# An attention kernel with a hand-made plan: the value groupings of its windowed half go by DMA on the SP queue instead of copies on VectorE, and eps is added as a per-row scalar

## The chip, the cores and the metric

The kernel runs on one core of one Trainium2 chip. The time is device microseconds (us) of that core. Three executions of the kernel before gave 351.57, 351.86 and 356.25 us; the median, 351.86 us, is the time to compare with. A further execution was profiled: it took 352.71 us, and 350.6 us of that is the span that the profile covers.

## The reference, cut to what matters

Two attention layers, A and B, work on a sequence of 2048 rows with D = 640, 32 heads and 20 values a head. Their results stand side by side in the output.

```
# A: causal softmax attention inside each of 4 segments of 512 rows,
#    and a memory (M, z) of the segments before
a_dot = softmax(q k^T * scale + causal mask) v
a_mem = (phi(q) M) / (phi(q) z + 1e-06)        # phi(t) = t + 1 if t > 0 else exp(t)
o = g * a_mem + (1 - g) * a_dot                # g = sigmoid(beta), one per head
M, z = M + phi(k)^T v, z + sum(phi(k))
# B: every row i looks at the rows j with 0 <= i - j < 256
o = softmax(where(mask, q k^T * scale, -1e9)) v
out = concat([o_A @ A_wo, o_B @ B_wo], axis=-1)
```

## The kernel before, in words

**Chunks.** The work is cut into eight chunks of 512 rows, in the order A0, B0, A1, B1, A2, B2, A3, B3. While the scores of one chunk run, the projections of the next one (q, k and v) are worked in between. Heads are taken four at a time: eight groups, 0 to 7.

**A chunk's path.** TensorE computes q and k (`qk_job`, line 416) and v (`v_job`, line 550) into two PSUM banks named `m`, and VectorE evicts them (lines 445, 568, 573). The last 12 rows of each quarter of q and k are regrouped through DRAM by DMAs on the SP queue (`regroup`, lines 400 and 408); they make the groups 5 to 7. Scores go to three PSUM pairs named `sc` (line 631), ScalarE turns them into `pt` tiles by exp (line 647; 12 such tiles in a ring), GpSimd zeroes what the mask excludes (line 682), or VectorE does, for the window's ends (line 664). TensorE multiplies by the values (lines 696 and 717), VectorE transposes the result (line 748), takes reciprocals (line 774), GpSimd divides (line 782). For A's memory, the denominators get eps added first (line 768), then a reciprocal (line 772), a product on VectorE (line 793) and a sum on GpSimd (line 802). The finished rows go to DRAM (line 820), come back transposed by DMA (line 835), are multiplied by wo (line 735) and stored (line 906).

**B's values.** A window of 256 rows makes a tile of 128 queries look at half a tile of keys at both ends. The halves of two different tiles are put together in one 128-row operand. For this, `v_ends` (line 583) makes three further groupings of the value tile `vB`: `vL` (the lower 64 partitions of four tiles), `vU` (the upper 64 partitions) and `vX` (the upper 64 of this chunk's first tile above the lower 64 of the last chunk's). It runs after each of the two halves of the heads, `half` 0 and 1: three VectorE copies each time, and for half 0 of a chunk that has one before it two more, that carry the last chunk's values over. This makes 30 copies in the program, all on line 601. `half` 0 covers the columns 0 to 335, `half` 1 the rest. Line 697 reads 32 columns from 21 h on for head h, so the last head of group 3 (h = 15) reads columns 315 to 346, and with them 11 of half 1.

**What sets the order.** The program has no loop at run time. A planner (`Flow`, line 58) keeps a clock of its own for every engine, adds the cost that each call states (`on_dve(402.0)`, for example), and issues at each point what its clocks say is ready. `when_idle` puts a VectorE job off until VectorE's planned time allows it; `at` issues at a planned time; `mark` says when a result is there, and the value product of a group waits, in the plan, for the mark "v" of that group (lines 1157 and 1160). Each engine then runs its instructions strictly in the planned order, with semaphores for the true dependences. A change of one stated cost so can move instructions on every engine. DMAs are spread over eight completion semaphores; one that reuses a semaphore waits until the earlier transfer on it has landed (the planner's `LANES`, line 47).

Of the kernel before, what the change touches and what calls it, by code (L numbers as in the profile page):

```python
# [9 lines left out]
ALU = mybir.AluOpType  # L10
# [3 lines left out]
P = 128  # L14
H = 32
DH = 20
# [168 lines left out]
class _K:  # L185
# [397 lines left out]
    def v_ends(self, n, c, half, v):  # L583


        f = self.f
        lo, hi = slice(0, SH), slice(SH, P)
        w = 16 * VS
        s = slice(0, w) if half == 0 else slice(w, VW)
        todo = []  # L590
        if half == 0 and c > 0:
            pv = self.vB[(c - 1) % 2]
            todo += [(self.vU[hi, 0:2, :], pv[hi, 2:4, :], 580.0),
                     (self.vX[lo, :], pv[lo, 0, :], 380.0)]
        todo += [(self.vL[lo, :, s], v[lo, :, s], 610.0),
                 (self.vU[hi, 2:4, s], v[hi, 0:2, s], 320.0),
                 (self.vX[hi, s], v[hi, 0, s], 430.0)]
        left = [len(todo)]
        for out, in_, ns in todo:
            def go(out=out, in_=in_, ns=ns):  # L600
                self.nc.vector.tensor_copy(out=out, in_=in_)
                t = f.on_dve(ns)
                left[0] -= 1
                if left[0] == 0:
                    for g in range(4 * half, 4 * half + 4):
                        self.mark(t, n, "v", g)
            f.when_idle(f.dve + 138.0, go)

    def v_tile(self, name, now=True):
        v = self.big.tile([P, LT, VW], BF16, name=name)  # L610
# [142 lines left out]
    def norm(self, turned, dst, add_to, last, g=None):  # L753


        nc, f = self.nc, self.f
        tt, slot, t0 = turned
        NB = L // HD
        tv = tt[:].rearrange("p (b c) -> p b c", c=HD)
        rr, rslot = self.piece("rr", NTT, 1, F32, (P, NB))  # L760
        a, b = tv[:, :, 0:DH], rr[:].unsqueeze(2).to_broadcast([P, NB, DH])
        if len(dst.shape) == 4:
            a = a.rearrange("p (g b) d -> p g b d", g=4)
            b = b.rearrange("p (g b) d -> p g b d", g=4)

        def s1():
            if add_to:
                nc.vector.tensor_tensor(out=rr[:], in0=tv[:, :, DH],
                                        in1=self.eps[:, g:g + 1].to_broadcast([P, NB]),
                                        op=ALU.add)  # L770
                f.on_dve(100.0, t0)
                nc.vector.reciprocal(out=rr[:], in_=rr[:])
            else:
                nc.vector.reciprocal(out=rr[:], in_=tv[:, :, DH])  # L774
            t1 = f.on_dve(276.0, t0)
            if add_to:
                f.when_idle(t1, lambda: s3(t1))
            else:
                f.at(t1 - 100.0, lambda: s2(t1))

        def s2(t1):
            nc.gpsimd.tensor_tensor(out=dst, in0=a, in1=b, op=ALU.mult)  # L782
            t2 = f.on_pool(QPOOL, t1)
            self.done_with(slot, t2)
            self.done_with(rslot, t2)
            if last:
                last(t2)

        def s3(t1):
            while len(self.adds) >= 2:  # L790
                self.adds[0]()
            u, uslot = self.piece("u", 2, 1, BF16, (P, NB, DH))
            nc.vector.tensor_tensor(out=u[:], in0=a, in1=b, op=ALU.mult)
            t = f.on_dve(480.0, t1)
            self.done_with(slot, t)
            self.done_with(rslot, t)

            def add():
                if add not in self.adds:
                    return  # L800
                self.adds.remove(add)
                nc.gpsimd.tensor_tensor(out=dst, in0=dst, in1=u[:], op=ALU.add)  # L802
                t3 = f.on_pool(717.0, t)
                self.done_with(uslot, t3)
                if last:
                    last(t3)
            self.adds.append(add)
            f.at(t, add)

        f.when_idle(t0, s1)  # L810

    def final(self, n, o, scr, wo, out2d, r0, col, t0, t1, t):
# [549 lines left out]
```

## Time and profile before

| what | value |
|---|---|
| median of three executions | 351.86 us |
| profiled execution, its span | 352.71 us, 350.6 us |
| busy: PE / ACT / POOL / DVE | 326.4 / 315.0 / 294.3 / 278.2 us |
| exp on ACT (line 647) | 320 instructions, 296.6 us |
| value copies on DVE (line 601) | 30 instructions |
| eps added on DVE (line 768) | 24 instructions, 7.8 us |
| granted TensorE clock | 1.00 in every stretch |
| data moved by DMA | 40.54 MB, 45.2% of 16 engines' span on queue q1 |

PE is TensorE's matmuls, ACT is ScalarE, POOL is GpSimd, DVE is VectorE, SPq is the SP engine's queue, which issues nearly all DMAs. A busy PE is not one at its peak, since matmuls are pipelined. The durations of ACT rows overlap a little with the next row: in a run of exps their starts lie about 0.9 us apart (23 exps in the 20.00 us from 108 to 128), while one row reads 1.07 us on average. In the columns of a stretch, each engine's number is its busy time inside the stretch, with the instructions in brackets.

### The profile page before, as it was taken

To read this page: it belongs to the slowest core of one execution; us is meant where nothing else is said; L and a number is where in the kernel's file an instruction comes from. 1 tells how busy PE (TensorE), PEld (TensorE's weight loads), DVE (VectorE), ACT (ScalarE), POOL (GpSimd) and SP (SyncE) were. 2 spreads that over 40 slices of the span, in tenths; PEclk is the share of its full clock that TensorE was granted. 3 is DMA by queue.
4 is the path that set the end of the run, shared out by engine and by line. 5 is a ranking of instruction groups with operands and counts; after the bars stand their busy time and mean duration, and the time that the engine had idled before them with its cause. 6 is when DMAs were issued, how large, how long until landed. Compare 5 with 4: busy or idle time off the path is not lost.

```text
span 350.6 us, 13578 instructions
## 1 busy us (share of the span) xinstructions
PE 326.4 (93%) x5617; PEld 167.0 (48%) x5617; DVE 278.2 (79%) x557; ACT 315.0 (90%) x358; POOL 294.3 (84%) x592
## 2 busy tenths in 40 slices
PE   7999999989999999999999999988999999899994
PEld 2443435444544345455644436454543445566672
DVE  5687677999958999999967998997867999766621
ACT  2897499999999999999999999999999999989831
POOL 6589388988898989999898989899988989987720
PEclk9999999999999999999999999999999999999999
DMA  7945617526675133033794025030483032675773
GB/s 233 376 159 129 165 32 227 128 64 178 200 124 123 22 77 122 2 93 69 175 193 104 0 63 155 3 79 8 82 143 77 2 75 61 146 140 150 146 183 115
DMA packets 69374, 40.54 MB, mean 116 GB/s; under 512 B 48448, under 2 KB 67520, under 8 KB 69312
## 3 DMA queue, kind: packets, MB, share of 16 engines
q1 hardware_dynamic: 67584, 38.35, 45.2%
q10 hardware_dynamic: 1728, 1.32, 1.2%
q8 instruction: 44, 0.72, 0.9%
q14 instruction: 18, 0.15, 0.1%
HBM read 16.06 MB, written 16.38 MB: 93 GB/s over the span
## 4 chain that ended last, share of the span: by engine, by line
PE 48%; DVE 22%; POOL 11%; issue 6%; ACT 5%; DMA 5%; SPq 2%; DVEq 0%; ACTq 0%; POOLq 0%
PE m L735 30%; PE sc L631 9%; POOL pt L682 7%; PE m L696 6%; ACT pt L647 5%; DVE tt L748 4%; DVE pt L664 3%; DMA xT<-in_B_x_dram 2%; PE m L717 2%; DMA scr_o<-o 2%; POOL o L782 2%; DVE kB L445 1%; PE sc L735 1%; DVE pq L471 1%; DVE qA L445 1%
## 5 line engine op out<-in xcount | busy, mean ns | idle before, releaser
L647 ACT ACTIVATE pt<-sc 128x1024 bf16<-128x1024 f32 (+1 forms) x320 | 296.6, 1070 | 14.9 <-PE sc L631 12.9
L682 POOL TENSOR_SCALAR_AFFINE_SELECT pt<-pt 128x256 bf16<-128x256 bf16 x448 | 209.6, 495 | 36.0 <-ACT pt L647 30.8
L748 DVE STREAM_TRANSPOSE tt<-m 128x512 f32<-128x512 f32 x88 | 60.7, 706 | 19.4 <-PE m L696 9.4
L782 POOL TENSOR_TENSOR o<-tt,rr 128x320 bf16<-128x320 f32 x64 | 51.2, 801 | 2.8 <-DVE rr L774 2.7
L631 PE MATMUL sc<-qB,kB 20*64 20x64 bf16 (+2 forms) x1728 | 39.0, 217 | 1.2 <-issue 0.6
L735 PEld LDWEIGHTS <-xT 128*128 128x128 bf16 x320 | 28.7, 97 | 22.4 <-issue 11.6
L735 PEld LDWEIGHTS <-oT 128*128 128x128 bf16 x320 | 28.8, 97 | 17.2 <-issue 3.5
L631 PE MATMUL sc<-qA,kA 20*128 20x128 bf16 (+3 forms) x512 | 36.1, 300 | 0.9 <-ACT pt L647 0.3
L631 PEld LDWEIGHTS <-kB 20*64 20x64 bf16 (+1 forms) x1728 | 21.7, 98 | 25.1 <-issue 23.1
L735 PE MATMUL m<-wv_A,xT 128*128 128x320 bf16 x160 | 27.4, 300 | 3.7 <-DVE kA L445 2.0
L891 DVE CAST ot<-m 128x320 bf16<-128x320 f32 x46 | 21.9, 480 | 8.5 <-PE m L735 8.3
L735 PE MATMUL m<-xT,wq_A 128*128 128x512 bf16 x100 | 26.6, 386 | 1.1 <-DVE qA L445 0.9
L664 DVE TENSOR_TENSOR pt<-pt,ends 128x1024 bf16<-128x1024 bf16 x32 | 27.6, 875 | 0.0
L735 PE MATMUL m<-xT,wk_A 128*128 128x512 bf16 x100 | 27.2, 392 | 0.3
L735 PE MATMUL m<-xT,wBq 128*128 128x512 bf16 x100 | 25.8, 380 | 1.2 <-DVE tt L748 1.2
L735 PE MATMUL m<-xT,wBk 128*128 128x512 bf16 x100 | 25.3, 381 | 0.6 <-DVE kB L445 0.6
L735 PE MATMUL m<-wBv,xT 128*128 128x320 bf16 x160 | 25.6, 300 | 0.3 <-DVE tt L748 0.2
L631 PEld LDWEIGHTS <-kA 20*128 20x128 bf16 x512 | 10.5, 91 | 30.5 <-issue 29.8
L696 PE MATMUL m<-pt,vA 128*32 128x128 bf16 (+3 forms) x512 | 24.0, 302 | 0.5 <-POOL pt L682 0.3
L735 PE MATMUL m<-wo_A,oT 128*128 128x320 bf16 x120 | 20.8, 300 | 0.2 <-DVE ot L891 0.2
L802 POOL TENSOR_TENSOR o<-o,u 128x320 bf16<-128x320 bf16 x24 | 20.5, 854 | 0.0
L445 DVE CAST qB<-m 128x512 bf16<-128x512 f32 x20 | 13.6, 682 | 7.4 <-PE m L735 7.4
(87 smaller groups left out, 427.7 us busy)
## 6 DMA issues: line engine op xcount, KB each, us to landing
scr_o<-o SPq DMA_DIRECT2D x28, 160.0 KB
out_dram<-ot SPq DMA_DIRECT2D x27, 160.0 KB
xT<-in_B_x_dram SPq DMA_DIRECT2D x4, 720.0 KB
scr_pk<-e SPq DMA_DIRECT2D x15, 128.0 KB
xT<-in_A_x_dram SPq DMA_DIRECT2D x3, 640.0 KB
scr_kA<-kA SPq DMA_DIRECT2D x16, 60.0 KB
scr_qA<-qA SPq DMA_DIRECT2D x16, 60.0 KB
kA<-scr_kA SPq DMA_DIRECT2D x16, 60.0 KB
```

Of the source, the lines that this page charges most:

```text
L445: nc.vector.tensor_copy(out=dst[:, m, at:at + L], in_=ps[:, :])
L631: nc.tensor.matmul(ps[j // 2][h0:h1, j % 2, c0:c0 + nq], lhsT=k[rows, g, kc + h0:kc + h1], rhs=q[rows, g, q0:q0 + nq], start=True, stop=Tr ...
L647: nc.scalar.activation(out=pt[:, :, lo:hi], in_=ps[i][:, :, lo:hi], func=ACT.Exp, scale=self.scale)
L664: nc.vector.tensor_tensor(out=blk, in0=blk, in1=self.ends[:].unsqueeze(1).to_broadcast([P, 1024 // SH, SH]), op=ALU.mult)
L682: nc.gpsimd.affine_select(out=blk, in_=blk, pattern=pat, compare_op=ALU.is_ge, fill=self.zero, base=base, channel_multiplier=mul)
L696: nc.tensor.matmul(O[HD * j:HD * j + HD, q0:q0 + nq], lhsT=v[:, VS * h:VS * h + HD], rhs=pts[j // 2][:, j % 2, c0:c0 + nq], start=(n_ == 0 ...
L717: nc.tensor.matmul(O[HD * j:HD * j + HD, o0:o0 + nq], lhsT=v[:, VS * h:VS * h + HD], rhs=pts[j // 2][:, j % 2, c0:c0 + nq], start=(n_ == 0 ...
L735: self.nc.tensor.matmul(ps[:, 0:n], lhsT=lhsT, rhs=rhs, start=start, stop=stop)
L748: self.nc.vector.transpose(out=tt[:], in_=O[:, :])
L782: nc.gpsimd.tensor_tensor(out=dst, in0=a, in1=b, op=ALU.mult)
L802: nc.gpsimd.tensor_tensor(out=dst, in0=dst, in1=u[:], op=ALU.add)
L891: nc.vector.tensor_copy(out=ot[:, 320 * hf:320 * hf + 320], in_=ps[:, 0:320])
```

## The change

In `v_ends`, the copies on VectorE become DMAs from SBUF to SBUF on the SP queue. All of one half are issued together, at the planned time at which VectorE has evicted the values; the order inside is now `vL`, `vU`, `vX`, and the two carried pieces last. The mark "v" is set from the planned landing of the last DMA. In `norm`, the eps of A's memory is no longer a tensor that is broadcast along the row, but the per-row scalar of a tensor_scalar; the planned cost stays 100 ns.

```diff
@@ v_ends @@
-        todo = []
+        todo = [(self.vL[lo, :, s], v[lo, :, s], 820.0),
+                (self.vU[hi, 2:4, s], v[hi, 0:2, s], 410.0),
+                (self.vX[hi, s], v[hi, 0, s], 205.0)]
         if half == 0 and c > 0:
             pv = self.vB[(c - 1) % 2]
-            todo += [(self.vU[hi, 0:2, :], pv[hi, 2:4, :], 580.0),
-                     (self.vX[lo, :], pv[lo, 0, :], 380.0)]
-        todo += [(self.vL[lo, :, s], v[lo, :, s], 610.0),
-                 (self.vU[hi, 2:4, s], v[hi, 0:2, s], 320.0),
-                 (self.vX[hi, s], v[hi, 0, s], 430.0)]
-        left = [len(todo)]
-        for out, in_, ns in todo:
-            def go(out=out, in_=in_, ns=ns):
-                self.nc.vector.tensor_copy(out=out, in_=in_)
-                t = f.on_dve(ns)
-                left[0] -= 1
-                if left[0] == 0:
-                    for g in range(4 * half, 4 * half + 4):
-                        self.mark(t, n, "v", g)
-            f.when_idle(f.dve + 138.0, go)
+            todo += [(self.vU[hi, 0:2, :], pv[hi, 2:4, :], 820.0),
+                     (self.vX[lo, :], pv[lo, 0, :], 410.0)]
+        t = f.dve + 138.0
+
+        def go():
+            for out, in_, ns in todo:
+                self.nc.sync.dma_start(out=out, in_=in_)
+                tl = f.on_dma(1, ns, t)
+            for g in range(4 * half, 4 * half + 4):
+                self.mark(tl, n, "v", g)
+        f.at(t, go)
@@ norm, s1 @@
             if add_to:
-                nc.vector.tensor_tensor(out=rr[:], in0=tv[:, :, DH],
-                                        in1=self.eps[:, g:g + 1].to_broadcast([P, NB]),
-                                        op=ALU.add)
+                nc.vector.tensor_scalar(out=rr[:], in0=tv[:, :, DH],
+                                        scalar1=self.eps[:, g:g + 1], scalar2=None,
+                                        op0=ALU.add)
                 f.on_dve(100.0, t0)
```

## The prediction, as it was put on record

> **What bounds the kernel now.** I read the page's busy shares first:
>
> ```profile
> PE 326.4 (93%) x5617; PEld 167.0 (48%) x5617; DVE 278.2 (79%) x557; ACT 315.0 (90%) x358; POOL 294.3 (84%) x592
> ```
>
> Four engines are near each other, so the shares decide nothing. The second view is the table by stretches: from the first exp of B0 (41.14) to the end of the last exp (332.03), then the places where the 30 copies lie, then the last chunk (columns: us, then busy time of PE, PEld, DVE, ACT, POOL).
>
> ```profile
> 41.14:332.03 290.89, 275.18 (x5183) 142.30 (x5182) 244.78 (x498) 284.53 (x321) 263.62 (x513) 1.00 0.44 100
> 116.00:124.00 8.00, 7.56 (x84) 2.66 (x82) 7.77 (x17) 8.00 (x10) 7.65 (x15) 1.00 0.22 33
> 131.00:137.00 6.00, 5.84 (x152) 3.87 (x148) 5.47 (x11) 6.00 (x7) 6.00 (x13) 1.00 0.61 188
> 199.00:204.00 5.00, 5.00 (x45) 1.79 (x46) 4.82 (x12) 5.00 (x7) 4.56 (x10) 1.00 0.04 5
> 212.00:217.00 5.00, 4.83 (x90) 2.87 (x87) 4.42 (x9) 5.00 (x7) 5.00 (x10) 1.00 0.76 221
> 277.00:282.00 5.00, 5.00 (x51) 1.83 (x48) 4.82 (x11) 5.00 (x6) 4.45 (x10) 1.00 0.00 0
> 290.00:297.00 7.00, 6.92 (x160) 3.91 (x160) 6.32 (x14) 7.00 (x8) 7.00 (x15) 1.00 0.21 63
> 301.00:332.00 31.00, 28.71 (x935) 19.00 (x928) 19.93 (x42) 28.88 (x31) 25.25 (x57) 1.00 0.71 158
> ```
>
> ScalarE is busy 284.53 of 290.89 us and 36.00 of the 36.00 us of the six stretches with copies. It is the bound. Its work (320 exps, 30 exps for phi) is untouched by the change, and its idle time between 41.14 and 332.03 is 290.89 - 284.53 = 6.36 us. That is all a faster VectorE can give back there. VectorE itself is nearly full in the copy stretches (7.77 of 8.00, 4.82 of 5.00), which makes the copies look dear; but it isn't what ScalarE waits for.
>
> The third view is the chain that ended last, in its last 20 us (start, length, what):
>
> ```profile
> 333.53 0.80 PE m L717 x63
> 334.32 1.48 PE sc L735 x10
> ...
> 338.58 0.57 SPq L820
> ...
> 339.19 2.50 DMA scr_o<-o
> ...
> 341.81 3.49 DMA oT<-scr_o
> ...
> 345.35 1.54 PE sc L735 x10
> ```
>
> After the last exp the end is a chain of the SP queue: transposes of the last chunk's first three tiles, then the last rows' store, their transpose, ten matmuls. The fourth view is the SP queue in the last A chunk, where the new DMAs go:
>
> ```profile
> 281.21 1.55 SPq L400 DMA_DIRECT2D scr_kB<-kB  x4
> 285.34 1.42 SPq L408 DMA_DIRECT2D kB<-scr_kB  x4
> 286.80 1.64 SPq L400 DMA_DIRECT2D scr_qB<-qB  x4
> 290.65 1.42 SPq L408 DMA_DIRECT2D qB<-scr_qB  x4
> 294.13 5.03 SPq L906 DMA_DIRECT2D out_dram<-ot  x2
> ```
>
> The queue is idle for most of that time. By the waits of the queue, line 400 waited 15.6 us here for the last value copy.
>
> **The change, part by part.**
>
> *Copies removed.* The groups by shape have two ends among the copies:
>
> ```profile
> L601 DVE COPY vU<-vB 64x1368 bf16<-64x1368 bf16 x3 | 1.9, 648 | 0.1
> ...
> L601 DVE COPY vX<-vB 64x336 bf16<-64x336 bf16 x4 | 1.0, 245 | 0.1
> ```
>
> The eight shapes sum to 2.3 + 2.3 + 2.0 + 1.9 + 1.9 + 1.8 + 1.8 + 1.0 = 15.0 us of VectorE. What hides them is ScalarE's exps: it has no idle time in these stretches. If that cover were gone, the 15.0 us would show in full. Worth on the path: at most 6.36 us (all of ScalarE's idle time from 41.14 on), and at least nothing; it could not make things worse by itself. I take -0.5, near the lower end, since the only idle of ScalarE around copies is that of the stretch from 128 to 165 (36.29 busy of 37.00: 0.7 us).
>
> *Eps.* 24 tensor_tensors of 323 ns (7.8 us) become tensor_scalars. The nearest rows are line 352 (128x32, 172 ns) and line 467 (128x512 bf16, 371 ns). So VectorE gains 24 x 0.15 = 3.6 us or loses 24 x 0.05 = 1.2. They lie in the A chunks beside saturated exps: taken 0 on the path, ends -0.7 (the same idle) and +1.2 (if nothing hid the loss).
>
> *DMAs added on SP.* 30 issues: 2 x 3 for B0 and 2 x 3 + 2 for each of the other three. The queue's issues above take 1.55/4 = 0.39 us each, so 12 us of SP, in gaps of 4 to 16 us. Data: each half has 64 x 7 pieces of 672 to 696 bytes, 0.30 MB, and the carried pieces 0.26 MB three times; 3.2 MB in all beside 40.54 MB. Landing: the stores of line 400 end their issue at 282.76 and the next line that needs them starts at 285.34, so 2.6 us. What waits for them: in the changed order half 0 stands before the stores of kB (line 400), half 1 after the return of qB. In the last chunk half 1 is issued from 292.07 on, for 3 x 0.39 us, and lands at about 292.07 + 1.2 + 2.6 = 295.9; its first reader on PE runs at 301.31, 5.4 us later, and in B0 to B2 it is no tighter (group 0 needs only half 0; first readers at 65.4, 142.7, 224.0). B0's half 1 is now queued behind the 720 KB load of xT, which takes until 63.6 by the chain; it lands at about 66, and group 3, its first reader, comes some 10 us later. Half 0 is no later than its cast; line 400, queued behind it, waited for the last copy before and now waits for the cast only, some 2 us sooner, against 5 x 0.39 = 2.0 us of issues that fall into its wait. Taken 0; ends -0.7 and +4.1 (the first rival).
>
> On the SBUF page of the Trainium skill ("SBUF — State Buffer", Door 1) a rule speaks against such transfers: 64 partitions reach only 8 of the 16 ports, and 196 GB/s was measured on partitions 0 to 63. An estimate by it and by the fixed 2.0 us of "DMA: Bandwidth & Descriptors" (Anatomy of one DMA) is 0.30 MB / 196 GB/s + 2.0 = 3.5 us in place of the 2.6 us of this trace. The sum is the same by both, since 5.4 us are there; no run here has yet shown a 64-partition transfer.
>
> *Order.* The planner now sees less VectorE time and shifts matmuls between neighbouring score batches from about 58.6 us on (the first: a set of 84-wide matmuls now ahead of the 64 end scores). Instruction counts on PE, ACT and POOL stay equal. What such a plan costs is unknown. Nearest row: the longest wait of an exp for PE after 41.14 is 1.01 us, at 308.32. Ends: -6.36 (all idle gone) and +7.1 (one such wait more in each of the seven chunks after A0). I take 0, the middle of errors of both signs.
>
> *Tail.* In the changed order, five matmuls of the chunk before last stand after the last value product. The first of the three transposes reuses the buffer that they read, and so waits for them: 334.32 + 5 x 0.148 = 335.1, where before it was issued at 334.62 (by then a store of line 906, now moved behind, had held the queue until 334.53). From there the chain above is the same: +0.5. Ends -0.7 (if the moved store counts and PE's wait of 1.41 us before 345.35 covers the five) and +1.5 (two times the five matmuls).
>
> Sum: -0.5 + 0 + 0 + 0 + 0.5 = 0.0 against the profiled execution's 352.71. The median of the runs is 0.85 us below that; I predict 352.3, between the two.
>
> **The rivals.**
>
> *Slower: the regrouping of q and k is pushed back by the transfers ahead of it.* Place: last chunk. Its 64-wide scores of all eight groups start at 295.09 and need the q rows issued until 292.07, landing at 294.7: 0.4 us of slack (in the other chunks these scores come for two groups at a time, so groups 5 to 7 are needed late). Five transfers now precede the kB stores. If the stores are issued more than 0.4 us later than at 281.21, PE stands still and ScalarE after it. Price: 5 x 0.39 us of issues plus 0.56 MB at 221 GB/s (the rate of the stretch 212 to 217), 2.5 us, less 0.4: up to +4.1, so 356.8. For it: line 400 waited for the last copy. Against: the casts of kB come earlier.
>
> *Slower: the new order.* ScalarE's feed has three PSUM pairs and is paid for in waits of 0.2 to 1.0 us. If the order adds one wait of 1.01 us in each of seven chunks: +7.1, 359.8; from three such waits on it outweighs the rest. For it: the order was made with costs in which a transfer takes 205 to 820 ns, which nothing in the trace confirms. Against: the same planner made the order before, with 6.36 us of idle.
>
> *Faster: VectorE matters more than ScalarE's busy time shows.* If the freed 15.0 + 3.6 us of VectorE let PE run ahead and remove most of the waits: -5, 347.7. For it: PE waits on VectorE's evictions at many small places. Against: it can't pass 6.36 us, and none of that lies in the copies' stretches.
>
> **How the numbers follow.** No change within a few us (350 to 355): 0.53. Regrouping late (354 to 357): 0.12. Order (355 to 362): 0.19, of it 0.14 above +2%, that is above 358.9. VectorE (345 to 350): 0.13, of it 0.04 below -2%, that is below 344.8. 0.03 is left for things unseen, 0.01 of it faster by over 2%, 0.02 slower. So: faster 0.05, same 0.79, slower 0.16. 2% is about what a measurement of this kernel can tell from no change. The range 347.5 to 359.0 leaves out about 0.05 below and 0.15 above; the likeliest case alone has 350 to 355.
>
> **What would show it right or wrong.** Right: no line 601 on VectorE, its busy time near 260 us, ScalarE busy some 284 of 291 us as before, 15 to 19 us from the last exp to the end, SP waits at line 601 that nobody waits for. Wrong: waits of PE on value transfers; the end scores of the last chunk later than 295; new waits of exps for PE of over 1 us; or a ScalarE idle time well below 6 us.

## The result, and the profile after

The changed kernel took 355.75 us (median of 20 executions), the kernel before 352.51 us beside it (20). The ratio is 1.0083, with a 95% interval of 1.0062 to 1.0105: no change by the 2% that the prediction counts with, but 0.8% slower beyond doubt. The forecast of 352.3 us is 3.45 us below it; its range of 347.5 to 359.0 holds the time.

The profiled execution of the changed kernel took 357.28 us, 1.5 us above its median, with a span of 355.5 us. Line numbers behind line 601 are smaller by 2. First the busy shares and the row of the exps from the page; the last line is the row of the exps from the page of before.

```profile
PE 330.0 (93%) x5617; PEld 167.8 (47%) x5617; DVE 267.7 (75%) x526; ACT 314.7 (89%) x358; POOL 288.2 (81%) x592
...
L645 ACT ACTIVATE pt<-sc 128x1024 bf16<-128x1024 f32 (+1 forms) x320 | 296.3, 1081 | 18.9 <-PE sc L629 18.4
...
L647 ACT ACTIVATE pt<-sc 128x1024 bf16<-128x1024 f32 (+1 forms) x320 | 296.6, 1070 | 14.9 <-PE sc L631 12.9
```

The exps are as long as before (296.3 against 296.6 us). What grew is the idle time before them: 18.9 us, of which 18.4 for scores of PE, in place of 14.9 and 12.9. The table by stretches (us, busy time of PE, PEld, DVE, ACT, POOL, granted clock, DMA share, GB/s), the first row again from the first exp of B0 to the end of the last exp:

```profile
41.68:335.99 294.31, 278.26 (x5179) 142.62 (x5179) 234.14 (x467) 284.19 (x321) 257.40 (x513) 0.99 0.46 109
...
131.00:137.00 6.00, 6.00 (x96) 3.52 (x95) 5.88 (x14) 6.00 (x8) 5.31 (x11) 1.00 0.41 98
172.00:178.00 6.00, 4.16 (x144) 2.77 (x142) 5.22 (x10) 4.52 (x5) 4.76 (x9) 1.00 0.79 207
178.00:184.00 6.00, 6.00 (x89) 2.78 (x88) 2.80 (x8) 4.53 (x5) 3.02 (x7) 0.72 0.70 194
...
212.00:217.00 5.00, 5.00 (x67) 2.36 (x67) 4.04 (x11) 5.00 (x7) 4.90 (x10) 1.00 0.42 89
...
319.00:326.00 7.00, 5.55 (x162) 3.54 (x145) 4.18 (x9) 5.50 (x6) 3.94 (x10) 1.00 0.62 161
```

ScalarE is busy 284.19 us there (284.53 before), but in 294.31 us: 10.12 us idle, where 6.36 were. Where the copies used to lie it is still full (6.00 of 6.00, 5.00 of 5.00). The new idle time is mainly at three places, which its timeline shows (start, length, what, in brackets the idle time before it):

```profile
72.33 1.94 ACT L645 ACTIVATE pt<-sc 128x1024 bf16<-128x1024 f32 x2 [1.30 <-PE sc L629]
...
178.80 1.94 ACT L645 ACTIVATE pt<-sc 128x1024 bf16<-128x1024 f32 x2 [1.95 <-PE sc L629]
...
324.27 6.70 ACT L645 ACTIVATE pt<-sc 128x1024 bf16<-128x1024 f32 x7 [1.27 <-PE sc L629]
```

What held the scores up at 178.80 stands in the chain of waits:

```profile
174.97 0.43 PE m L733 x2
175.40 1.66 issue
177.06 1.11 PE m L733 x7
```

After two of nine matmuls of one group PE stands still for 1.66 us, and the profile knows no releaser ("issue"): there is no tile, semaphore or DMA that the third matmul lacks and the second had. At 322.42 the same happens for 1.45 us, after eight of sixteen scores. The third place, 72.33, has only a small break ahead of it, 0.29 us long, after 33 of 64 end scores. Both stand in PE's timeline:

```profile
71.85 0.33 PE L629 MATMUL sc<-qB,kB 20*64 20x64 bf16 x31 [0.29 <-issue]
...
323.86 0.29 PE L629 MATMUL sc<-qB,kB 20*128 20x128 bf16 x8 [1.45 <-issue]
```

Before 72.33, PE had also waited 0.81 us, up to 65.74, for an eviction of qA that VectorE did only after a mask of 2.10 us. That one execution is above the median. In e2, the run below with the same order, the break at 174.68 is 0.72 us, the one at 319.37 is 1.44, the one near 71 is missing, and the three waits are 0.87, 0.83 and 1.27 us.

The new transfers on the SP queue, in the last A chunk:

```profile
279.93 0.63 SPq L601 DMA_DIRECT2D vL<-vB  x1
280.61 0.93 SPq L601 DMA_DIRECT2D vU<-vB  x1
281.58 0.60 SPq L601 DMA_DIRECT2D vX<-vB  x1
```

And the end, again from the chain of waits:

```profile
335.34 2.14 PE sc L733 x15
...
344.19 4.94 DMA out_dram<-ot
350.12 1.53 PE sc L733 x10
```

From the first exp of B0 on the two profiles compare like this: 294.31 against 290.89 us to the end of the last exp (+3.42), and 19.55 against 18.60 us from there to the end (+0.95). The first exp of B0 itself is 0.54 us later. Together that is the 4.9 us by which the spans differ.

### The profile page after: what moved, and what is told of

Same layout as the page of the kernel before. It is cut to its first block, busy times and chain, and to the rows that moved or that the text cites. A ratio compares the mean times of both kernels' runs of the same rounds, so it can differ in the third digit from the quotient of the medians.

```text
span 355.5 us, 13588 instructions
## 1 busy us (share of the span) xinstructions
PE 330.0 (93%) x5617; PEld 167.8 (47%) x5617; DVE 267.7 (75%) x526; ACT 314.7 (89%) x358; POOL 288.2 (81%) x592
## 4 chain that ended last, share of the span: by engine, by line
PE 41%; POOL 21%; DVE 13%; ACT 11%; issue 6%; DMA 6%; SPq 2%; ACTq 0%; DVEq 0%; POOLq 0%
PE m L733 25%; POOL pt L680 13%; ACT pt L645 10%; PE sc L629 9%; PE m L694 4%; POOL o L780 3%; DMA wk_A<-in_A_wk_dram 2%; DVE pt L662 2%; POOL o L800 2%; PE m L715 2%; DVE tt L746 2%; POOL MZ L545 1%; DMA out_dram<-ot 1%; DVE vA L568 1%; PE sc L733 1%
## 5 line engine op out<-in xcount | busy, mean ns | idle before, releaser
L645 ACT ACTIVATE pt<-sc 128x1024 bf16<-128x1024 f32 (+1 forms) x320 | 296.3, 1081 | 18.9 <-PE sc L629 18.4
L780 POOL TENSOR_TENSOR o<-tt,rr 128x320 bf16<-128x320 f32 x64 | 48.5, 759 | 5.3 <-DVE rr L772 5.2
L629 PE MATMUL sc<-qB,kB 20*64 20x64 bf16 (+2 forms) x1728 | 40.7, 217 | 2.7 <-issue 2.0
L629 PE MATMUL sc<-qA,kA 20*128 20x128 bf16 (+3 forms) x512 | 36.9, 302 | 0.9 <-ACT pt L645 0.2
L889 DVE CAST ot<-m 128x320 bf16<-128x320 f32 x44 | 21.1, 483 | 13.1 <-PE m L733 11.9
L733 PE MATMUL m<-wo_B,oT 128*128 128x320 bf16 x100 | 18.7, 315 | 2.1 <-issue 1.7
```

The lines of the kernel that those rows point to most:

```text
L629: nc.tensor.matmul(ps[j // 2][h0:h1, j % 2, c0:c0 + nq], lhsT=k[rows, g, kc + h0:kc + h1], rhs=q[rows, g, q0:q0 + nq], start=True, stop=Tr ...
L645: nc.scalar.activation(out=pt[:, :, lo:hi], in_=ps[i][:, :, lo:hi], func=ACT.Exp, scale=self.scale)
L733: self.nc.tensor.matmul(ps[:, 0:n], lhsT=lhsT, rhs=rhs, start=start, stop=stop)
L889: nc.vector.tensor_copy(out=ot[:, 320 * hf:320 * hf + 320], in_=ps[:, 0:320])
```

## The experiments

Two theories came out of this. Theory A: the operations cost nothing, the new order of PE does. Its rival, theory B: the transfers themselves cost the time. Later a third came up, theory S: it is not what the order makes PE wait for, but where PE's supply of instructions breaks. The times beside the kernel before, by ratio:

| run | operations | order on PE | us | ratio | 95% interval |
|---|---|---|---|---|---|
| e1_eps_only | copies, scalar eps | before | 352.49 | 1.0012 | 0.9990 to 1.0033 |
| e3_transfers_old_plan | transfers, tensor eps | before | 350.82 | 0.9979 | 0.9957 to 1.0001 |
| e2_transfers_only | transfers, tensor eps | after | 353.88 | 1.0074 | 1.0052 to 1.0097 |
| e4_copies_new_plan | copies, scalar eps | after | 364.98 | 1.0383 | 1.0358 to 1.0408 |
| p_before | plain DMAs | before | 349.81 | 0.9956 | 0.9934 to 0.9979 |
| p_before_pad32 | and 32 matmuls | before | 353.56 | 1.0038 | 1.0007 to 1.0068 |
| p_before_pad | and 64 matmuls | before | 353.38 | 1.0057 | 1.0036 to 1.0078 |
| p_before_pad128 | and 128 matmuls | before | 351.78 | 1.0002 | 0.9978 to 1.0026 |
| p_after | plain DMAs | after | 353.77 | 1.0073 | 1.0042 to 1.0103 |
| p_after_pad32 | and 32 matmuls | after | 353.72 | 1.0041 | 1.0009 to 1.0072 |
| p_after_pad | and 64 matmuls | after | 353.91 | 1.0061 | 1.0030 to 1.0091 |
| p_oT3 | plain DMAs, third oT | after | 354.56 | 1.0054 | 1.0023 to 1.0084 |

The kernels named p_ leave the DMA transposes out, so they don't do the whole computation; they serve to compare one with another. Both edits together in the old order were not measured.

**The edits taken apart.** e1_eps_only is the kernel before with the eps edit alone.

```diff
-                nc.vector.tensor_tensor(out=rr[:], in0=tv[:, :, DH],
-                                        in1=self.eps[:, g:g + 1].to_broadcast([P, NB]),
-                                        op=ALU.add)
+                nc.vector.tensor_scalar(out=rr[:], in0=tv[:, :, DH],
+                                        scalar1=self.eps[:, g:g + 1], scalar2=None,
+                                        op0=ALU.add)
```

> The kernel before with only the eps addition changed; every engine keeps its order. All theories: ratio to before 0.998 to 1.002, VectorE's busy time down by 0 to 3.6 us (24 instructions). If eps carries the slowdown instead: 1.006 or more.

Measured 1.0012 [0.9990, 1.0033]. The new instruction is a little longer than the old one (376 ns here and 374 in the changed kernel, against 323), and nothing comes of it. From its groups by shape:

```profile
L768 DVE TENSOR_SCALAR rr<-tt,eps 128x16 f32<-128x16 f32 x24 | 9.0, 376 | 0.0
```

e2_transfers_only is the changed kernel with the old eps instruction, the diff above the other way round; every engine has the order of the changed kernel.

> The changed kernel with the old eps addition; the order is the changed one. If the transfers or the order they bring cost the time: ratio 1.006 to 1.011, as for the whole change. If eps does: 0.998 to 1.002.

Measured 1.0074 [1.0052, 1.0097]: the loss goes with the transfers or with the order that comes with them.

e3_transfers_old_plan is the kernel before with the transfers in place of the copies, one for one, while the planner is still told of VectorE copies. PE, ScalarE and GpSimd keep the order of before.

```diff
             def go(out=out, in_=in_, ns=ns):
-                self.nc.vector.tensor_copy(out=out, in_=in_)
+                self.nc.sync.dma_start(out=out, in_=in_)
                 t = f.on_dve(ns)
```

> The 30 transfers on the SP queue, but the planner is told the old VectorE costs, so that PE, ACT and POOL keep the order of before instruction for instruction. Theory A (the order costs the time: PE runs out of instructions at other places and waits more): ratio 0.994 to 1.002. Theory B (the transfers themselves cost it, through the SP queue or the DMA engines): 1.006 to 1.012.

Measured 0.9979 [0.9957, 1.0001]. The same 30 transfers, in the old order, cost nothing. VectorE falls from 278.2 to 263.5 us on the page:

```profile
PE 328.4 (94%) x5617; PEld 167.7 (48%) x5617; DVE 263.5 (75%) x527; ACT 314.2 (90%) x358; POOL 290.7 (83%) x592
```

e4_copies_new_plan is the counterpart: the changed kernel with copies for the transfers, while the planner is told of transfers.

```diff
             for out, in_, ns in todo:
-                self.nc.sync.dma_start(out=out, in_=in_)
+                self.nc.vector.tensor_copy(out=out, in_=in_)
                 tl = f.on_dma(1, ns, t)
```

> The order of the changed kernel on PE, ACT and POOL, but the 30 groupings are done by VectorE copies again; the planner does not know of their time. Theory A (order): 1.006 to 1.020, since the copies come on top. Theory B (transfers): 0.998 to 1.003.

Measured 1.0383 [1.0358, 1.0408], more than the order alone, and more than the 1.020 that theory A allowed at most. Five copies now stand in a row on VectorE, ahead of an eviction that PE needs. VectorE's timeline, and then ScalarE's:

```profile
117.40 0.70 DVE L601 COPY vL<-vB 64x1344 bf16<-64x1344 bf16 x1
...
120.16 0.67 DVE L601 COPY vX<-vB 64x684 bf16<-64x684 bf16 x1
120.75 1.27 DVE L445 CAST kB<-m 128x512 bf16<-128x512 f32 x2
```

```profile
122.96 1.94 ACT L645 ACTIVATE pt<-sc 128x1024 bf16<-128x1024 f32 x2 [1.93 <-PE sc L629]
```

The eviction of kB stands behind 3.35 us of copies, and the next exp waits 1.93 us. So these copies are hidden only where the planner spreads them out: transfers in place of copies are worth 3.0% in the order that has no room for copies (1.0383 against 1.0083), and 0.2% in the one that has (0.9979).

By these four, theory A stands against its rival: old order 1.001 and 0.998, new order 1.007 to 1.038. What in the order costs the 1% was still open.

**Where the instructions break off.** The trace also has PE's instruction transfers: 44 of 16 KB in the kernels before and after, some 255 of PE's 11,234 matmuls and weight loads each. The gap at 175.40 ends 1.36 us after one of them has landed, the gap at 322.42 1.35 us after another. If the gaps come from there, they move when the borders of the pieces move against the program. The next kernels move them. In all of them plain DMAs stand for the DMA transposes; with the transposes in place the borders were not moved.

```diff
-            nc.sync.dma_start_transpose(out=self.oT[n][:, :, t0 * P:t1 * P],
-                                        in_=scr[t0 * P:t1 * P, :])
+            nc.sync.dma_start(out=self.oT[n][:, :, t0 * P:t1 * P], in_=scr[t0 * P:t1 * P, :].rearrange(
+                "(p q) (u c) -> p (q u c)", p=P, c=P).rearrange("p (m x) -> p m x", m=self.KT))
```

> The kernel before, with its DMA transposes (lines 497 and 835) replaced by plain DMAs of the same bytes between the same tiles, so both outputs are made from values in another arrangement and the transposing itself is left out. It is the base for the three kernels beside it; orders on PE, ScalarE, VectorE and GpSimd are those of the kernel before. Expected by all theories: faster than the kernel before by 3 to 10 us (ratio 0.97 to 0.99), nearly all of it in the tail, where two transposes (3.9 us of issue, 3.5 us to land) lie on the chain.

Measured 0.9956 [0.9934, 0.9979], from the first exp of B0 to the last exp 288.78 us, from there to the end 17.02. The 3 to 10 us expected (ratio 0.97 to 0.99) did not come; the tail is 1.6 us shorter than before.

> The changed kernel with the same replacement of its DMA transposes by plain DMAs. Theory A (the order of PE costs the time): slower than the kernel before with the same replacement by 2 to 4.5 us, and again gaps of PE in the middle of a group near 175 and 322 us. Rival T (the loss comes from the SP queue, where the new transfers and the slow transposes meet): less than 1 us between the two.

Measured 1.0073 [1.0042, 1.0103]; 290.94 and 17.84 us. The loss by the new order is there without the transposes too (1.0073 / 0.9956 = 1.0118): rival T falls.

p_before_pad and p_after_pad have 64 more small matmuls in the warm-up, 128 instructions; nothing else moves on any engine.

```diff
+        [self.nc.tensor.matmul(ps[:, 0:32], lhsT=z[:, 0:P], rhs=z[:, 0:32], start=True, stop=True) for _ in range(64)]
         self.close(bi, f.seen)
```

> The kernel before with plain DMAs in place of the transposes and 64 further matmuls of 32 columns in the warm-up; their result is not read, and everything behind them is in the same order. PE fetches its instructions in pieces of 16 KB, some 255 instructions each, so 128 more move every border by half a piece against the program. Theory S (PE runs out of instructions where a border falls into a dense group): the gap of 1.04 us at 305.73 goes from there, others come elsewhere; the stretch from B0's first exp to the last exp changes by -1.5 to +2.5 us against the same kernel without the 64. Theory W (all gaps come from semaphores and buffers): gaps at the same instructions, the stretch equal within 0.5 us. By both the start may be 0 to 4 us later (64 matmuls at 0.04 to 0.06 us).

Measured 1.0057 [1.0036, 1.0078]: the old order loses 1.0% by 64 matmuls whose result is not read, and that put B0's first exp off by only 0.37 us. Here is the same place of the program in the timelines of PE, first without and then with the 64:

```profile
316.16 1.40 PE L735 MATMUL m<-wo_A,oT 128*128 128x320 bf16 x9
317.49 0.31 PE L631 MATMUL sc<-qB,kB 20*128 20x128 bf16 x4
318.05 0.35 PE L631 MATMUL sc<-qB,kB 20*128 20x128 bf16 x12 [0.24 <-issue]
```

```profile
316.47 0.20 PE L717 MATMUL m<-pt,vU 128*32 128x64 bf16 x2
317.91 0.21 PE L717 MATMUL m<-pt,vU 128*32 128x64 bf16 x2 [1.24 <-issue]
317.91 0.26 PE L717 MATMUL m<-pt,vB 128*32 128x128 bf16 x4
```

In the second, PE breaks off after 30 of a block of 64 value products (line 717). In the first it breaks off 64 matmuls later in the program: after the 64, one matmul of line 735, 16 scores, nine of line 735 and four scores, that is after 94. In the kernel before the break is at the same instruction, 0.64 us long, at 319.23.

> The changed kernel with plain DMAs in place of the transposes and the same 64 matmuls. Theory S: the gaps of PE inside the group of line 733 at 175.4 (1.66 us in the changed kernel) and inside the scores of line 629 at 322.4 (1.45 us) go from these two places or fall below 0.7 us, and with them the waits of exps that follow (1.95 and 1.27 us); others may come elsewhere. The stretch from B0's first exp to the last exp is 1 to 3 us shorter than without the 64. Theory W: both gaps stay with over 1 us at the same instruction, the stretch equal within 0.5 us. By both the start may be 0 to 4 us later.

Measured 1.0061 [1.0030, 1.0091]. Without the 64 and with them, different places:

```profile
319.25 0.37 PE L629 MATMUL sc<-qB,kB 20*128 20x128 bf16 x8
320.64 0.29 PE L629 MATMUL sc<-qB,kB 20*128 20x128 bf16 x8 [1.03 <-issue]
```

```profile
306.56 0.23 PE L629 MATMUL sc<-qB,kB 20*128 20x128 bf16 x4
310.66 0.51 PE L629 MATMUL sc<-qB,kB 20*128 20x128 bf16 x12 [3.87 <-issue]
```

The break at 319.62 is gone, and a longer one is there instead, 3.87 us: its piece began to be fetched only at 308.36, 1.56 us after PE had run out, in a stretch in which the DMA engines were 0.92 busy, and PE went on 1.37 us after it had landed. Theory W had the gaps stay where they were; they moved. Theory S had the stretch to the last exp 1 to 3 us shorter, which missed: in this profile it is 294.98 against 290.94 us, by the new break, while the median is the same. Where the borders fall is a draw for both orders.

With 128 matmuls, 256 instructions, the borders should be back on the same instructions.

> The kernel before with plain DMAs for the transposes and 128 further matmuls in the warm-up: 256 more instructions, one whole 16 KB piece, so that the pieces' borders fall on the same instructions as with none. Theory S: 0.9956 comes back but for the later start (0.37 us with 64, so up to 0.8 us with 128): ratio 0.994 to 1.000, and PE's gaps stand where they stand with none (no gap near 317). Rival X (it is the added work itself that cost the 1.0% that 64 matmuls cost: 0.9956 to 1.0057): 1.006 to 1.018, twice the loss or at least the same.

Measured 1.0002 [0.9978, 1.0026]. The start is 1.43 us later (B0's first exp at 42.84 against 41.42, where 0.8 us was the most expected), 0.4% of the time; less that, it is 0.9961, so what 64 cost is back. Rival X had at least 1.006. The break near 317 is gone:

```profile
318.92 1.40 PE L735 MATMUL m<-wo_A,oT 128*128 128x320 bf16 x9
320.25 0.57 PE L631 MATMUL sc<-qB,kB 20*128 20x128 bf16 x16
320.75 1.53 PE L735 MATMUL m<-wo_A,oT 128*128 128x320 bf16 x10
```

The small break of 0.24 us that p_before has after four of these sixteen scores did not come back either: a border there does not always cost a break.

> The kernel before with plain DMAs for the transposes and 32 further matmuls: the borders are moved by a quarter of a piece. Theory S: gaps of PE in further places, each ending 1.3 to 1.5 us after a piece has landed; the ratio lies anywhere from 0.993 to 1.008. Rival X: 1.000 to 1.001, half of what 64 cost.

Measured 1.0038 [1.0007, 1.0068], with the place that theory S asks for: 32 matmuls later than with 64, after 62 of the same 64 value products.

```profile
317.21 0.20 PE L717 MATMUL m<-pt,vU 128*32 128x64 bf16 x2
318.58 0.21 PE L717 MATMUL m<-pt,vU 128*32 128x64 bf16 x2 [1.17 <-issue]
```

> The changed kernel with plain DMAs for the transposes and 32 further matmuls. Theory S (where the borders fall decides most of the difference between the two orders): 0.998 to 1.012, and the difference to the kernel before with the same 32 matmuls may be anywhere from -0.5 to +1.2%; the mean difference over none, 32 and 64 matmuls is about +0.5%. Rival A (the new order itself costs its 1%, at any position of the borders): 0.9 to 1.3% above the kernel before with the same 32 matmuls.

Measured 1.0041 [1.0009, 1.0072]: 0.03% above the old order with the same 32 matmuls, where rival A had 0.9 to 1.3%. Its longest break is 2.44 us:

```profile
307.98 0.40 PE L629 MATMUL sc<-qB,kB 20*128 20x128 bf16 x11
310.82 0.28 PE L629 MATMUL sc<-qB,kB 20*128 20x128 bf16 x5 [2.44 <-issue]
```

So the new order stands 1.18% above the old one with no added matmuls, 0.03% with 32 and 0.04% with 64 (each about +-0.4%, the two intervals taken together). The mean is 0.4%, some 1.5 us.

A count over all fourteen profiles (before, after and the twelve runs of the table) says the same. From B0 on PE has 31 gaps of over 0.3 us that are put down to "issue". Counted in PEld's rows from the program's start, every one stands 100 to 102 rows behind a multiple of 128 (4708, 5093 and 5348 in the kernel before, 2532, 5094 and 5349 in the changed kernel, 5092 with 64 matmuls), whatever the instruction there computes, and 1.2 to 1.6 us after a piece has landed. 128 matmuls with their weight loads are 256 instructions, one piece.

**The tail.** p_oT3 is p_after with a third oT buffer.

```diff
-                self.oT[n] = self.big.tile([P, self.KT, L], BF16, name="oT", bufs=2)
+                self.oT[n] = self.big.tile([P, self.KT, L], BF16, name="oT", bufs=3)
```

> The changed kernel with plain DMAs for the transposes and a third oT buffer, so that the last chunk's first load of rows does not have to wait for the five matmuls of the chunk before that stand behind the last value product; the order of all instructions is the same. By the prediction's tail step the SP queue no longer stands idle before that load (from 334.66 to 335.60 with two buffers), the time from the last exp to the end falls from 17.84 us to 17.0 to 17.4, and the ratio from 1.0073 to 1.005 to 1.007. Rival (the end is set by another chain): tail and ratio unchanged.

Measured 1.0054 [1.0023, 1.0084], which does not stand apart from p_after's 1.0073, and 17.84 us from the last exp to the end, as with two buffers: the 17.0 to 17.4 us that the tail step had here missed, and the rival held. The load of the last chunk's first rows did come sooner. The SP queue of p_after, then of p_oT3:

```profile
335.60 1.99 SPq L833 DMA_DIRECT2D oT<-scr_o  x3
```

```profile
334.71 2.07 SPq L833 DMA_DIRECT2D oT<-scr_o  x3
```

But PE has the five matmuls and then 80 more to do without a break, so the five probably cost their own time there (17.84 against 17.02 us in p_before). With transposes, the buffer's part was not tried.

## Why the prediction was right, point by point

The verdict (no change by 2%) and the range held, but the likeliest case did not quite: it had 350 to 355 us, and 355.75 lies where the rival "the new order" had put its 355 to 362 us, at a chance of 0.19. Two of the signs of being wrong were seen: end scores later than 295, and new waits of exps for PE of over 1 us. The bound and the price of the edits on the path were right, the price of the order was not; the range held because it counted that rival in, at up to 7.1 us.

*The bound.* Right: ScalarE, 284.19 busy of 294.31 us, and full where the copies had been.

*Copies removed, and the transfers on SP.* Right on the path. Taken -0.5 and 0; together e3 measured -0.21% [-0.43, +0.01], -0.7 us. One size was off: 27 of the 30 issues take 0.54 to 0.72 us each (three others 0.93, 0.96 and 1.61) and not 0.39, so together they take 20 us of SP and not 12. All of it is hidden: no instruction of PE waited for a value transfer. The nearest row, 12-partition transfers, was no row for 64-partition ones. The estimate by the SBUF page's rule stays open, since nothing waited for a landing that would show it; its 2.0 us stands on the DMA page under the path of DMAs that GpSimd issues, and these are issued by SP.

*Eps.* Taken 0, right (1.0012 [0.9990, 1.0033]). Of its two ends the upper one was the true price, 24 x 0.05 = 1.2 us of VectorE, hidden. VectorE's busy time came out at 267.7 us and not near 260: 278.2 - 15.0 + 1.2 = 264.4, and a few masks and evictions read longer.

*Regrouping late (rival).* Fell. kB's stores go at 284.27 in place of 281.21 and the end scores start at 298.79 in place of 295.09, but the return of qB, issued until 295.10, is some 1.1 us ahead of them by the prediction's 2.6 us of landing, and PE has no wait for it. The sign "later than 295" was seen, but not by the regrouping: in e3, with the same transfers in the old order, the end scores start at 293.83. Here they come after the loss at 72 and 178 us.

*VectorE matters more (rival).* Fell: 14.7 us less of VectorE in e3 are worth 0.7 us.

*Tail.* Taken +0.5. The first transpose is issued 3.11 us after the last exp in place of 2.59: +0.52, right at the end of the five matmuls (339.06), and 3.11 again in e2, where e1 and e3 have 2.26 and 2.61 in the old order. The whole tail grew by 0.95 us. Behind the transposes the chain was not the same as before, as the step had it: it now goes through a store of line 904 at 344.19. But tails differ by execution, 18.04 us (e1), 18.60 and 19.03 (e3) in the old order, 19.40 (e2) and 19.55 in the new one, so not all of the 0.95 belongs to the order.

*Order.* This is the term that was mis-sized: "I take 0, the middle of errors of both signs". With the transfers fixed, e2 against e3, the new order costs 1.0074 against 0.9979, 1.0%, some 3.3 us. The rival "the new order" had the right place, waits of exps for PE, and three of them came (1.30, 1.95, 1.27 us). But it took such waits for a property of the order. Two of the three come from breaks in PE's instruction supply; of the third, 0.87 us stays in e2, where it has no break ahead of it. The trace of before already showed such breaks and the prediction did not read them: 1.04 us at 305.73 and 0.64 at 319.23, both in the middle of a group and both put down to "issue". From PE's timeline:

```profile
306.77 0.24 PE L717 MATMUL m<-pt,vX 128*32 128x128 bf16 x3 [1.04 <-issue]
...
319.88 0.35 PE L631 MATMUL sc<-qB,kB 20*128 20x128 bf16 x12 [0.64 <-issue]
```

The wait of 1.01 us at 308.32, which the prediction took as the price of a bad place in the order, comes right behind the first of them; p_before has neither that break nor a wait of an exp of over 0.2 us there. The borders fall well for the old order as it stands (0.9956, but 1.0038 and 1.0057 when moved), so a new order had something to lose; that is read from the kernels without transposes. What is left for the order itself is 0.4% in the mean of three positions, with the tail's 0.8 us in it. It includes things like PE's wait of 1.39 us at 142.98 for an eviction behind a mask of 2.32 us, where the old order waited 0.85 for the same tile. How that mean splits up further is not settled, and three positions are few.

None of the runs with the whole computation beats both kernels by more than its interval; the nearest is e3, the transfers in the old order (0.9979 [0.9957, 1.0001]).

## What to carry to other kernels

When an edit to a fully unrolled kernel also re-plans the order, time the operations in the old order and the order with the old operations: here the operations were worth -0.2% and the order +1.0%, and a verdict on the sum would have blamed the transfers. In the profile, read PE's gaps "<-issue" that split one group of equal matmuls: they are no dependence, and moving the program by half a piece (64 matmuls whose result is not read) shows whether a difference of 1% belongs to the edit or to where the pieces end. Here differences below 1% between two such programs meant little until that was tried.

## What the runs showed of the hardware

*Instruction supply.* With small matmuls back to back (64 end scores, then 64 value products, in 1.7 us), PE uses its instructions up faster than 16 KB pieces come: the fetch of one mostly takes 0.9 to 1.7 us, and PE goes on only 1.2 to 1.6 us after its landing. Breaks are 0.2 to 3.9 us long; they moved by exactly 32 and 64 matmuls when as many were added. The Trainium skill ("Runtime: NRT & Kernel Launch", Instruction fetch mechanics) calls the cost of crossing such a border "mostly hidden"; the runs agree with its 256 instructions a piece, and differ on the cost: moving the borders by 64 matmuls changed the time by 1.0% (0.9956 to 1.0057). Why the piece at 308.36 was fetched so late was not tried; the busy DMA engines are only a guess.

*The clock.* A break can cost twice. After the one of 1.66 us at 175.40 the granted clock is halved for 3.4 us:

```profile
174.80:178.20 3.40, 1.57 (x13) 0.88 (x17) 2.64 (x5) 2.04 (x3) 1.97 (x4) 1.00 0.71 147
178.20:181.60 3.40, 3.40 (x21) 1.27 (x18) 1.14 (x3) 2.29 (x3) 1.76 (x4) 0.50 1.07 286
```

PE was busy 1.57 of the 3.40 us before. The same followed the break of 2.44 us, for twice as long the one of 3.87 us, and in e3 a gap of 1.39 us before 305.69 (2.01 of 3.40 busy), which the profile puts down to a mask on GpSimd, though it too ends at a border, 1.41 us after a landing. The break of 1.45 us at 322.42 was not followed by it (1.96 of 3.40), so the busy share alone does not tell. One such stretch takes 0.005 off the mean granted clock of an execution. A mean of 0.995 or less was seen in 7 of 20 executions of the changed kernel, which took 356.8 us in the mean where the other 13 took 354.8; and in 1 of 12 of p_before, 7 of 12 with 64 matmuls more, 1 of 12 with 128. It is no mark of the new order alone: e1, in the old one, has 5 of 12. The Trainium skill ("TensorE: Matmul & The Clock Gate", What's actually happening) has a window of 3.4 us, which agrees, and asks for an idle window, which a half busy one is not.

*Issue cost.* A transfer from SBUF to SBUF over 64 partitions takes the SP queue mostly 0.60 to 0.64 us to issue, one of the 12-row stores of line 400 0.39 us.
